# A fused attention and mixture-of-experts kernel: the attention's pieces in another written order

## The chip, the cores and the metric

The kernel runs on one core of a Trainium2 chip. The metric is the device time of one execution in microseconds (us). A core has five engines, each with its own instruction stream that it works through in order: TensorE (PE; its weight loads are shown as PEld), VectorE (DVE), ScalarE (ACT), GpSimd (POOL) and SyncE (SP, which here issues most transfers).

## The reference, cut to what matters

Shapes: q, k and v are 8 batches x 8 heads x 576 tokens x 64. Attention has two parts that are added; the result, as 4608 rows of 512, goes through a mixture of 8 experts, one expert per row.

```python
# part 1: all against all, on means over 4 neighbouring tokens (144 of 576), repeated 4 times
out_d = sm_attn(q_d, k_d, v_d);  out_up = np.repeat(out_d, 4, axis=2)
# part 2: each token against those less than 4 away
scores = np.where(np.abs(pos[:, None] - pos[None, :]) < 4, scale * q @ k.T, -1e9)
out_local = softmax(scores) @ v
x = (out_up + out_local).transpose(0, 2, 1, 3).reshape(4608, 512)
# experts: logits, argmax, gate = softmax weight of the chosen one
e_idx = np.argmax(x @ w_gate + modality_bias[modality_id], axis=1)
out[rows of e] = gate * (np.maximum(x[rows of e] @ w1[e], 0) @ w2[e])
```

## The kernel before, in words

**Attention** (class `Attention`) works in 32 steps n, four per batch: a step is two of the batch's heads, as two halves of the partitions. Its pieces, by their names in the code, are: `tpq` and `tpk` transpose queries and keys on PE, `tpt` does the odd rest of two steps; `qT` and `kT_` copy them out of PSUM on ACT; `kd` sums the keys by fours on DVE, from the same PSUM tile that `kT_` copies; `qe` and `qd` sum the queries by fours on POOL. `mk` and `sc` put the mask and the local scores of half a step into PSUM, `lm` and `le` take the maximum and subtract it on DVE, `exp` is on ACT, `z` and `zr` sum and invert on DVE, `nl` normalises on POOL, `lt` transposes on DVE, the four `Pw_` copies on ACT write the block form, and `avl` multiplies by the values on PE. The coarse part has `scd`, `dm`, `de`, `nd`, `pdt`, `PdT`, `avd` and `Od`; `vp` and `vc` make its values. `X` adds both parts on DVE.

**Routing** (class `Router`) runs per batch, some three steps behind: `lg`, `LT`, `lgt`, `L`, `ch1`, `ex`, `ch2`, `gt`, `pr`, `pl`, the table scatters `st` on POOL's queue, the transposes `R` on DVE and their stores `W` on SP's queue.

**Experts** come last: units of gathered rows, two matrix products each. The first unit begins within the last attention steps.

What sets the order: `build` gives every piece a time, in steps, from the table `PHASE` (n + phase for a piece of step n, 4b + phase for a piece of batch b), sorts all calls by it and records them in that order under a manual schedule. Each engine then holds its instructions in that order, and waits where a tile is not ready. Loads of q, k and v are calls too; their places were worked out from other entries: a query and key load from the latest of the three transposes, a value load from the later `avl`. PSUM tiles stand in four small rings (3 buffers for `tp`, `tpt`, `vp`, `pdt`, `lgt`; 3 for `sc` and `scd`; 2 for `avd`, `avl`, `lg`, `pr`). After attention's last pieces another scheduler orders the expert stage.

Of the kernel before, what the change touches and what calls it, by code (L numbers as in the profile page):

```python
# [20 lines left out]
B, H, S, D = 8, 8, 576, 64  # L21
# [174 lines left out]
class Attention:  # L196
# [114 lines left out]
    def kd(s, n, i):  # L311
# [9 lines left out]
        else:  # L321
            p = s.t.pop(("tp", "k", n)).rearrange("m (t x) -> m t x", x=4)
# [154 lines left out]
class Router:  # L477
# [116 lines left out]
    def R(s, b, t):  # L594

        if t < s.t["G", b]:
            if t % 2 == 0:
# [586 lines left out]
def build(tc, q, k, v, mid, w_gate, bias, w1, w2, out):  # L1184
    nc = tc.nc
    with ExitStack() as ctx:
# [10 lines left out]
        with ExitStack() as actx:  # L1197
# [40 lines left out]
            last = max(P["tpq"], P["tpk"], P["tpt"])  # L1238
            used = max(P["avl0"], P["avl1"])
            batch = ("lg", "LT", "lgt", "L", "ch1", "ch2", "ex", "gt", "pr", "pl", "st", "R", "W")  # L1240
            for b in range(B):
                call(4 * b + min(P[x] for x in P if x[:2] in ("lg", "R0")), lambda b: ro.begin(b, X[b]), b)
            for nm, p in P.items():
                f, i = (nm[:-1], int(nm[-1])) if nm[-1].isdigit() and nm not in ("ch1", "ch2") else (nm, 0)
                if f in batch:
                    for b in range(B - 1):
                        late_ = {2: 0.05, 0: 0.9, 3: 0.14}.get(i, 0) if f == "st" and b == B - 2 else 0
                        call(4 * b + p + late_, getattr(ro, parts.get(f, f)), b, i)
# [339 lines left out]
```

## Time and profile before

| | |
|---|---|
| Median of 3 runs | 667.54 us (667.39 to 668.28) |
| The profiled execution, its own time | 669.48 us |
| Its span, first to last instruction | 667.8 us |
| Mean granted TensorE clock | 0.987 of full |
| Busy: PE, DVE, ACT, POOL | 624.9, 444.2, 387.2, 337.7 us |
| Attention ends (last X) | 256.0 us |

The span has three parts. Up to some 30 us the first loads arrive. The attention steps follow, up to 256 us. From there PE does expert matmuls to the end. A row of the trace gives an engine, a source line, an operation, and out<-in by the names above.

### The profile page before, as it was taken

To read this page: it belongs to the slowest core of one execution; us is meant where nothing else is said; L and a number is where in the kernel's file an instruction comes from. 1 tells how busy PE (TensorE), PEld (TensorE's weight loads), DVE (VectorE), ACT (ScalarE), POOL (GpSimd) and SP (SyncE) were. 2 spreads that over 40 slices of the span, in tenths; PEclk is the share of its full clock that TensorE was granted. 3 is DMA by queue.
4 is the path that set the end of the run, shared out by engine and by line. 5 is a ranking of instruction groups with operands and counts; after the bars stand their busy time and mean duration, and the time that the engine had idled before them with its cause. 6 is when DMAs were issued, how large, how long until landed. Compare 5 with 4: busy or idle time off the path is not lost. (4 is left out here: it accounts for less than half of the span.)

```text
span 667.8 us, 16270 instructions
## 1 busy us (share of the span) xinstructions
PE 624.9 (94%) x5987; PEld 493.9 (74%) x5987; DVE 444.2 (67%) x977; ACT 387.2 (58%) x902; POOL 337.7 (51%) x376
## 2 busy tenths in 40 slices
PE   6798989987998879999999999999999999999996
PEld 4566666765766657888888888888888888889894
DVE  7688898989898985744346673766737967225540
ACT  5698989987898862422354642446324464335540
POOL 7544645627376747343049876498764730113102
PEclk9899999998999997999999999999999999999998
DMA  9999898798899856277002435234341234537801
GB/s 183 164 183 185 162 181 178 153 195 166 171 157 218 165 148 153 87 177 187 16 32 103 107 85 161 53 103 107 90 155 68 79 111 143 173 111 204 242 1 45
DMA packets 178012, 90.21 MB, mean 135 GB/s; under 512 B 144036, under 2 KB 162506, under 8 KB 177930
## 3 DMA queue, kind: packets, MB, share of 16 engines
q1 hardware_dynamic: 169994, 69.96, 48.7%
q0 software_dynamic: 7936, 19.18, 9.3%
q8 instruction: 48, 0.79, 0.6%
q14 instruction: 34, 0.28, 0.2%
HBM read 69.86 MB, written 19.51 MB: 134 GB/s over the span
## 5 line engine op out<-in xcount | busy, mean ns | idle before, releaser
L1045 PE MATMUL l<-V,H 128*128 128x512 f32 x804 | 190.0, 395 | 0.0
L1045 PEld LDWEIGHTS l<-V,H 128*128 128x128 f32 x804 | 150.2, 188 | 34.7
L923 POOL DMA_INDIRECT xg<-xs,m x64 | 74.8, 1169 | 19.2 <-issue 18.6
L405 POOL TENSOR_TENSOR le<-le,zr 128x384 f32<-128x384 f32 x32 | 26.7, 834 | 88.8 <-DVE zr L401 76.8
L1055 POOL DMA_INDIRECT out_dram<-o,tq x24 | 28.7, 1194 | 79.9 <-ACT o L1047 61.9
L992 PE MATMUL l<-X,H 128*128 128x512 f32 (+1 forms) x264 | 58.9, 375 | 0.0
L421 ACT COPY Pw<-lt 32x288 f32<-32x288 f32 x128 | 54.6, 426 | 3.7 <-DVE lt L416 2.1
L1047 ACT ACTIVATE o<-l,tq 128x512 f32<-128x512 f32 x24 | 16.5, 689 | 68.6 <-PE l L1045 43.7
L992 PEld LDWEIGHTS l<-X,H 128*128 128x128 f32 x264 | 45.7, 193 | 9.2 <-issue 1.0
L621 POOL DMA_INDIRECT tab<-ig,si x36 | 38.7, 1075 | 19.0 <-DVE pn L745 12.8
L1148 ACT ACTIVATE H<-o 128x512 fp32r<-128x512 f32 x36 | 22.8, 634 | 39.7 <-DVE o L1170 39.6
L460 PE MATMUL avl<-Pw,vw 128*64 128x96 f32 x768 | 40.2, 254 | 5.7 <-ACT Pw L421 5.6
L460 PEld LDWEIGHTS avl<-Pw,vw 128*64 128x64 f32 x768 | 33.6, 139 | 13.6 <-ACT Pw L421 8.3
L1055 POOL DMA_INDIRECT out_dram<-o,tg x12 | 13.6, 1137 | 55.7 <-ACT o L1047 40.1
L860 DVE TENSOR_TENSOR V<-raw,V 128x1024 fp32r<-128x1024 f32 x23 | 34.4, 1512 | 7.1 <-ACT V L854 7.0
L391 ACT ACTIVATE de<-scd,dm 128x144 f32<-128x144 f32 x96 | 35.4, 377 | 5.4 <-DVE dm L383 3.4
L309 ACT COPY kT<-tp 64x512 f32<-64x512 f32 x64 | 37.0, 579 | 2.4 <-PE tp L277 1.6
L997 ACT ACTIVATE H<-l 128x512 fp32r<-128x512 f32 x24 | 14.4, 598 | 36.5 <-PE l L992 36.0
L998 DVE SCALAR_TENSOR_TENSOR H<-l,H 128x512 fp32r<-128x512 f32 x24 | 16.5, 690 | 28.5 <-ACT H L997 28.4
L351 PE MATMUL sc<-kT,qT 128*24 128x64 f32 x1536 | 34.5, 223 | 1.0 <-ACT kT L309 1.0
L351 PEld LDWEIGHTS sc<-kT,qT 128*24 128x24 f32 x1536 | 24.5, 103 | 11.0 <-issue 4.6
L378 PE MATMUL scd<-kd,qd 64*64 64x144 f32 x384 | 31.1, 295 | 1.4 <-DVE le L364 1.4
(277 smaller groups left out, 1421.2 us busy)
## 6 DMA issues: line engine op xcount, KB each, us to landing
raw<-in_moe_w_dram SPq DMA_DIRECT2D x112, 128.0 KB
raw<-in_moe_w_dram SPq DMA_DIRECT2D x28, 512.0 KB
vw<-in_v_dram SPq DMA_DIRECT2D x60, 180.0 KB
qt<-in_q_dram SPq DMA_DIRECT2D x30, 288.0 KB
kt<-in_k_dram SPq DMA_DIRECT2D x30, 288.0 KB
xs<-R SPq DMA_DIRECT2D x56, 128.0 KB
xs<-G SPq DMA_DIRECT2D x8, 128.0 KB
xg<-xs,m POOLq DMA_INDIRECT x64, 3.0
```

Source lines behind the costliest of these rows:

```text
L309: s.nc.scalar.copy(s.kB[r, g, a, PAD + 64 * g : PAD + 64 * g + 512], p[r])
L351: s.nc.tensor.matmul(p[32 * j : 32 * j + SUB, 2 * i : 2 * i + 2, :], qT[:, q0 : q0 + SUB], kB[:, :, q0 : q0 + WIN], start=False, stop=(i = ...
L378: s.nc.tensor.matmul(p[r, c, :], qd[r, 40 * c : 40 * c + 64], kd[r, :], start=True, stop=True, skip_group_check=True)
L391: s.nc.scalar.activation(x, s.t["scd", n][:, c].rearrange("p (k x) -> p k x", k=NB), AF.Exp, bias=m[:, c : c + 1], accum_out=s.t["z", n][: ...
L421: s.nc.scalar.copy(s.Pw[n % NPW][r, :, j, :SUB], s.t["lt", n][r, :, :SUB])
L460: s.nc.tensor.matmul(p[64 * a : 64 * a + 64, c], vw[:, NB * (4 * (hp // 2) + hp % 2 + 2 * a) + k, :], Pw[:, 2 * k + a], start=True, stop=T ...
L621: i = nc.gpsimd.indirect_dma_start(out=s.tab[:, :], out_offset=bass.IndirectOffsetOnAxis(ap=C.si[:, t : t + 1], axis=0), in_=C.ig[:, t, :] ...
L860: (nc.gpsimd if turn == 4 else nc.vector).tensor_tensor(lo, raw, hi.bitcast(F32), op=ALU.subtract)
L923: s.nc.gpsimd.indirect_dma_start(out=R[l].rearrange("p h (i x) -> p (h i) x", i=4)[:, i, :], out_offset=None, in_=s.xs.rearrange("n (a x) ...
L992: nc.tensor.matmul(p[:, f % n, :], a[:, fs], x[:, k, :N], start=(k == 0 and i == 0), stop=(k == 3 and i == 2))
L1045: nc.tensor.matmul(p, l, x[:, f % 2, :], start=(f == 0 and i == 0), stop=(f == 7 and i == 2))
L1055: nc.gpsimd.indirect_dma_start(out=s.out[:, :], out_offset=bass.IndirectOffsetOnAxis(ap=T[:, h, 0:1], axis=0), in_=o, in_offset=None, boun ...
```

## The change

The table `PHASE` holds new numbers for every piece. Three rules of `build` go with it. The loads have entries `qk` and `v` of their own, with the values that were worked out before (0.4388 and 3.8377). The scatters of the last batch but one are placed by `nd`, `nl` and `pl`. A batch's first use is found over `lg` and all `R`. In `kd` the tile is no longer taken out of the dictionary, so that `kd` may be written before `kT_`; in `R` the tile of two transposes is made by whichever comes first. Both programs hold the same instructions in the same number.

```diff
 PHASE = {
-    "tpq": 0.0000, "tpk": 0.0000, "qT0": 0.0000, "mk0": 0.0000, "tpt": 0.1888, "kT0": 0.2050, "qT1": 0.5097,
...
+    "tpq": 0.0000, "tpk": 0.0054, "tpt": 0.0286, "kd0": 0.0860, "qT0": 0.1020, "kT0": 0.1281, "qT1": 0.3104,
...
 }
...
-            p = s.t.pop(("tp", "k", n)).rearrange("m (t x) -> m t x", x=4)
+            p = s.t["tp", "k", n].rearrange("m (t x) -> m t x", x=4)
...
-            if t % 2 == 0:
+            if ("R", b, t // 2) not in s.t:
...
-            last = max(P["tpq"], P["tpk"], P["tpt"])
...
-                call(4 * b + min(P[x] for x in P if x[:2] in ("lg", "R0")), lambda b: ro.begin(b, X[b]), b)
+                call(4 * b + min(P[x] for x in P if x[:2] == "lg" or x[0] == "R"), lambda b: ro.begin(b, X[b]), b)
...
-                        late_ = {2: 0.05, 0: 0.9, 3: 0.14}.get(i, 0) if f == "st" and b == B - 2 else 0
-                        call(4 * b + p + late_, getattr(ro, parts.get(f, f)), b, i)
+                        at_ = 4 * b + p
+                        if f == "st" and b == B - 2:
+                            at_ = {2: max(N - 2 + P["nd"], 4 * b + P["pl"]) + 0.0001, 0: N - 1 + P["nl"] + 0.0001, 3: N - 0.865 + P["nd"]}.get(i, N + 2.2)
+                        call(at_, getattr(ro, parts.get(f, f)), b, i)
...
-                        call(4 * b - 1 + used + 0.3 + 0.8 * j, at.load_v, b + 1, 4 * j)
+                        call(4 * b - 1 + P["v"] + 0.8 * j, at.load_v, b + 1, 4 * j)
...
-                call(2 * h - 5 + last + 0.25, at.load_qk, h // 2, h % 2)
+                call(2 * h - 5 + P["qk"], at.load_qk, h // 2, h % 2)
```

Line numbers after the table are one higher in the changed kernel. DVE in the step in which the routing of the batch before runs, from the reciprocal of the sums (`zr`) to the first routing piece (`L`), before:

```order
L401 RECIPROCAL zr<-zr 128x15
L606 STREAM_TRANSPOSE R<-X 128x512
L323 TENSOR_REDUCE kd<-tp 128x128
L358 TENSOR_REDUCE lm<-sc 128x6
L364 TENSOR_TENSOR le<-sc,lm 128x192
L526 TENSOR_REDUCE L<-lgt 128x16 x2
```

and in the changed kernel:

```order
L607 STREAM_TRANSPOSE R<-X 128x512
L401 TENSOR_SCALAR zr<-z 128x15
L402 RECIPROCAL zr<-zr 128x15
L365 TENSOR_TENSOR le<-sc,lm 128x192
L324 TENSOR_REDUCE kd<-tp 128x128
L359 TENSOR_REDUCE lm<-sc 128x6
L417 STREAM_TRANSPOSE lt<-le 128x384
L527 TENSOR_REDUCE L<-lgt 128x16 x2
L365 TENSOR_TENSOR le<-sc,lm 128x192
```

Here `R` moved ahead of the sums, the first `le` moved between the reciprocal and `kd`, and `lt` ahead of the second `le`; a maximum and its subtraction no longer stand next to each other.

ACT in the same step, from the queries' copy (`qT`) to the exponentials of the scores (`le<-le`), before:

```order
L297 ACTIVATE qT<-tp 128x512
L514 COPY LT<-lg 128x256
L309 COPY kT<-tp 64x512 x2
L514 COPY LT<-lg 128x256
L421 COPY Pw_166<-lt 32x12x24 x3
L450 ACTIVATE Od<-avd 128x144
L540 ACTIVATE ex<-L 128x32
L369 ACTIVATE le<-le 128x384
```

and in the changed kernel:

```order
L515 COPY LT<-lg 128x256 x2
L422 COPY Pw_166<-lt 32x12x24
L298 ACTIVATE qT<-tp 128x512
L310 COPY kT<-tp 64x512 x2
L422 COPY Pw_166<-lt 32x12x24
L541 ACTIVATE ex<-L 128x32
L451 ACTIVATE Od<-avd 128x144
L422 COPY Pw_167<-lt 32x12x24
L370 ACTIVATE le<-le 128x384
```

Both `LT` copies moved ahead of `qT`, and two of the three `Pw` copies that stood behind `kT` moved ahead of `qT`.

PE in the same step, from the mask (`sc<-mask`) ahead of the router's logits (`lg`) to the local values (`avl`), before:

```order
L343 MATMUL sc<-mask,identb 128x192
L507 MATMUL lg<-X,wg 32x256 x8
L351 MATMUL sc<-kT,qT 24x64 x12
L520 MATMUL lgt<-ident,LT 128x128 x4
L445 MATMUL avd<-PdT,vd 64x144 x4
L378 MATMUL scd<-kd,qd 64x144 x6
```

and in the changed kernel:

```order
L508 MATMUL lg<-X,wg 32x256 x8
L278 MATMUL tp<-ident,qt 128x128 x4
L278 MATMUL tp<-ident,kt 128x128 x4
L344 LDWEIGHTS identb
L344 MATMUL sc<-mask,identb 128x192
L352 MATMUL sc<-kT,qT 24x64 x12
L521 MATMUL lgt<-ident,LT 128x128 x4
L379 MATMUL scd<-kd,qd 64x144 x6
L446 MATMUL avd<-PdT,vd 64x144 x4
```

`lg` moved ahead of the step's transposes, so that these and a mask stand between `lg` and `lgt`, and `scd` moved ahead of `avd`.

## Rows read from the trace of the kernel before

**Rows 1.** The page: busy time by engine; the table scatters (busy, mean ns, idle before)

```profile
PE 624.9 (94%) x5987; PEld 493.9 (74%) x5987; DVE 444.2 (67%) x977; ACT 387.2 (58%) x902; POOL 337.7 (51%) x376
...
L621 POOL DMA_INDIRECT tab<-ig,si x36 | 38.7, 1075 | 19.0 <-DVE pn L745 12.8
```

**Rows 2.** Busy time by stretch; columns: stretch, its length, busy us by engine, clock, DMA

```profile
30.43:60.07 29.64, 26.07 (x511) 19.34 (x512) 24.06 (x75) 26.37 (x85) 11.70 (x18) 1.00 0.99 190
60.07:88.57 28.50, 26.01 (x516) 19.36 (x513) 25.15 (x79) 25.95 (x82) 15.34 (x20) 1.00 0.96 168
88.57:117.11 28.54, 25.69 (x513) 19.26 (x510) 25.63 (x81) 25.73 (x82) 16.52 (x22) 1.00 0.90 180
117.11:145.82 28.71, 26.20 (x516) 19.49 (x513) 25.29 (x79) 25.98 (x82) 15.19 (x20) 1.00 0.85 169
145.82:178.68 32.86, 27.12 (x511) 20.35 (x510) 29.73 (x105) 25.94 (x81) 16.48 (x22) 0.95 0.94 176
178.68:207.16 28.48, 26.07 (x516) 19.33 (x513) 25.30 (x79) 25.89 (x82) 19.41 (x24) 1.00 0.94 181
207.16:227.66 20.50, 18.52 (x374) 14.02 (x371) 19.11 (x57) 18.53 (x59) 15.97 (x18) 1.00 0.94 162
227.66:256.00 28.34, 22.17 (x329) 15.82 (x328) 22.48 (x64) 17.94 (x53) 15.83 (x17) 0.91 0.63 151
256.00:668.00 412.00, 405.22 (x1901) 332.58 (x1899) 225.93 (x312) 177.37 (x251) 190.83 (x165) 0.99 0.39 112
```

**Rows 3.** Busy time by step of one cycle; order of engines: PE, PEld, DVE, ACT, POOL

```profile
178.68:185.16 6.48, 6.42 (x132) 4.89 (x129) 6.24 (x23) 5.77 (x20) 3.40 (x4) 1.00 0.81 172
185.16:191.30 6.14, 5.50 (x116) 4.22 (x115) 5.90 (x17) 5.92 (x18) 4.93 (x7) 1.00 1.03 161
191.30:197.78 6.48, 6.48 (x129) 4.80 (x129) 5.64 (x15) 6.32 (x22) 4.44 (x7) 1.00 0.66 119
197.78:207.16 9.38, 7.66 (x143) 5.42 (x144) 7.52 (x27) 7.88 (x26) 6.63 (x8) 1.00 1.15 243
```

**Rows 4.** Waits from 178.68 to 207.16: us in total, times, longest

```profile
DVE kd L323 <- ACT kT L309: 2.0, 2, 1.4
...
ACT LT L514 <- PE lg L507: 0.8, 1, 0.8
ACT qT L297 <- PE tp L277: 0.6, 1, 0.6
...
PE lgt L520 <- ACT LT L514: 0.9, 1, 0.9
PE pr L572 <- DVE late L471: 0.7, 1, 0.7
```

**Rows 5.** DVE in order of time, behind the routing step's kd: start, us, line, operation

```profile
202.23 0.35 DVE L358 TENSOR_REDUCE lm<-sc 128x6 f32<-128x192 f32 x1
...
207.13 0.70 DVE L606 STREAM_TRANSPOSE R<-X 128x512 f32<-128x512 f32 x1
...
209.22 0.19 DVE L584 TENSOR_TENSOR sl<-pr,ecap 128x40 f32<-128x40 f32 x1
...
210.35 0.65 DVE L606 STREAM_TRANSPOSE R<-X 128x512 f32<-128x512 f32 x1
210.92 0.65 DVE L323 TENSOR_REDUCE kd<-tp 128x128 f32<-128x512 f32 x1
```

**Rows 6.** Busy time from one kT to the next, and ACT's second LT in it

```profile
200.41:208.34 7.93, 6.40 (x131) 5.04 (x123) 6.38 (x23) 6.50 (x20) 4.34 (x6) 1.00 1.18 251
...
201.61 0.43 ACT L514 COPY LT<-lg 128x320 f32<-128x320 f32 x1
```

**Rows 7.** Busy time in the stretch at half clock

```profile
251.20:258.00 6.80, 6.49 (x33) 4.83 (x34) 3.19 (x7) 1.04 (x3) 6.55 (x5) 0.50 0.46 92
```

**Rows 8.** SP's issue of a pair's query load, and PE's first use of it

```profile
148.88 1.20 SPq L233 DMA_DIRECT2D qt<-in_q_dram  x2
...
178.68 0.60 PE L277 MATMUL tp<-ident,qt 128*128 128x128 f32 x4
```

More of the change, by code (lines that the diff above doesn't have):

```diff
@@ L1241, in build @@
             for b in range(B):
-                call(4 * b + min(P[x] for x in P if x[:2] in ("lg", "R0")), lambda b: ro.begin(b, X[b]), b)
+                call(4 * b + min(P[x] for x in P if x[:2] == "lg" or x[0] == "R"), lambda b: ro.begin(b, X[b]), b)
             for nm, p in P.items():
+                if nm in ("qk", "v"):
+                    continue
                 f, i = (nm[:-1], int(nm[-1])) if nm[-1].isdigit() and nm not in ("ch1", "ch2") else (nm, 0)
```

19 rows, old and new, of the table PHASE are left out of this document.

## The prediction

> **What bounds the kernel now.** I read the page's busy shares first, then busy time by stretch, then one cycle of the attention stage step by step, then the waits of that cycle. The page gives PE 94% of the span [rows 1], which looks like a bound engine. The stretches say where that holds: from 256 us on the routed-expert stage keeps PE busy nearly throughout, and the table that changes holds no piece of it. Before that lie the 32 attention steps, and in them three engines stand close together: over the four steps from 178.68 to 207.16 DVE is busy 25.30, ACT 25.89 and PE 26.07 of 28.48 us [rows 2]. No engine is full; each loses 2.4 to 3.2 us per four steps to waits for the other two. So the order of work, and not an amount of work, sets the length of this stage, and what the stage gives back goes straight to the end, because PE works without a break behind it.
>
> The four steps are not alike [rows 3]. The first three take 6.48, 6.14 and 6.48 us with at most 0.84 us of idle DVE or 0.71 of idle ACT. The fourth, in which the routing of an earlier batch runs, takes 9.38 us with DVE busy 7.52 and ACT 7.88: there the time is lost.
>
> How much can go? If in each step the busier of DVE and ACT had no wait, the cycle would be 6.24 + 5.92 + 6.32 + 7.88 = 26.36 us, so its room is 28.48 - 26.36 = 2.12 us [rows 3]. I leave PE out of that sum. In the third step its busy time is the whole step, 6.48 of 6.48, while its weight loads take 4.80 [rows 3]; its matmuls are pipelined and their ends are modelled. Counting PE too, the sum is 6.42 + 5.92 + 6.48 + 7.88 = 26.70 and the room 1.78. The Trainium skill, "Perfetto Trace Analysis", section "Identifying the Most-Contended Engine", says that matmul busy time is a bad measure of how near TensorE is to its limit and that weight-load busy time is a better one; by that rule 2.12 is the room; with PE counted it is 1.78, and the forecast below would be 2.3 us higher. The trace agrees with the rule as far as 4.80 of 6.48 goes.
>
> For all seven stretches from 30.43 to 227.66 the time that the busiest of DVE and ACT stands idle is 3.27, 2.55, 2.81, 2.73, 3.13, 2.59 and 1.39, together 18.5 us [rows 2]. Scaled as in the cycle above (2.12 of 2.59) this is **15.1 us** of room.
>
> **The change, part by part.** No instruction is added or removed; both programs hold the same ones, so busy time stays, and only waits can come and go.
>
> *kd ahead of kT.* Both read the transposed keys of one PSUM tile, and the second reader waits for the first. Before, DVE's kd stood behind ACT's two kT copies and waited 2.0 us per cycle, 1.4 of it in the routing step [rows 4]. Now kd stands before kT, and DVE's wait goes. The price is that kT waits for kd. In the three plain steps I cost this at nothing: ACT has qT ahead of kT, and now two Pw copies ahead of qT, while DVE is the less busy of the two in two of them (5.90 against 5.92, 5.64 against 6.32) [rows 3]. If this cover is gone, each kT waits for at most one whole kd, 0.65 us [rows 5].
>
> *The routing step on DVE.* From the end of one kd to the end of the next DVE works without a wait from 202.23 to 210.92 + 0.65 = 211.57, that is 9.34 us [rows 5]. The change takes out of this interval the two R transposes (0.70 and 0.65) and the four sl and si pieces (4 x 0.19 = 0.76), which now stand behind the next kd or before this one: 7.23 us are left. ACT's work from kT to kT is 6.50 us, less one LT copy of 0.43 that now stands before qT: 6.07 [rows 6]. So ACT will wait some 7.23 - 6.07 = **1.16 us** for kd once per cycle. This is the new wait.
>
> *LT together.* Before, ACT wrote one LT, then the two kT copies, then the other LT, and PE's second pair of lgt transposes waited 0.9 us with avd, scd and avl queued behind it [rows 4]. Now the LT copies follow each other and PE has both tp groups, a mask and a score group between lg and lgt. The lgt wait goes. ACT's 0.8 for lg may stay; it lies in the step where DVE is last, so I take the larger of this and the 1.16, not both.
>
> *pr later.* Before, PE's pr stood ahead of the next step's transposes and waited 0.7 us for DVE, and ACT's qT waited 0.6 behind it [rows 4]. Now pr stands behind tp, mk and tpt, a quarter of a step later. Both waits go; what is late next is DVE itself, which is the 1.16 again.
>
> *POOL.* The score normalisation nl and nd now come some 0.4 of a step earlier against pdt, and the table scatters have moved to either side of them. POOL is busy 19.41 of 28.48 us even in the cycle that also holds gathers [rows 2], so I cost the scatters at nothing. If one met an nl that was due, DVE's lt would wait up to its 1.08 us [rows 1], once a cycle.
>
> *Loads and stores on SP.* The two load offsets now have entries of their own, with the sums that were computed before (0.1888 + 0.25 and 3.5377 + 0.3), so the loads keep their place in the step. A pair's query load is issued at 148.88 and used at 178.68 [rows 8]: 30 us of cover, of which the forecast uses less than a microsecond per cycle. Two of the R transposes are written 0.2 of a step later and three earlier; the last store of a batch comes one and a half steps earlier, right behind its transposes. SP will wait there for DVE, with the next loads queued behind it under the same cover, so I cost this at nothing.
>
> *Ends.* The first 30 us wait for the first loads; I take no gain. The last stretch, 227.66 to 256, has 22.48 us of DVE work in 28.34 and mixes the last steps with the first expert matmuls; the pieces there move too, in no clear direction: 0, with 2 us to either side.
>
> **The sum.** Per cycle: room 2.12 less the new wait 1.16 is 0.96 us. Seven stretches, the last three quarters of a cycle long, are 6.75 cycles: 6.75 x 0.96 = 6.5 us. The profiled execution took 669.48 us by its own time, so 663.0 on its scale; it lies 1.94 above the median of the runs shown, 667.54, and on the median's scale the forecast is **661.0 us**. The bounds: all the room goes and the 1.16 hides under DVE, 667.54 - 15.1 = 652.4; or as many waits come as go, 667.5.
>
> **The rivals.**
>
> *All the room goes*, 652.4 us. For it: in the routing step DVE is last, and a wait of ACT there costs nothing if the buffers let ACT catch up in the next three steps. Against: in the third step ACT has 0.16 us of idle time [rows 3], so nothing can be caught up there.
>
> *The waits only change places*, 667.5 us. For it: kd behind kT becomes kT behind kd, and three engines at 90% leave little slack. Against: four different waits of the routing step [rows 4] are taken up at once, and only one new one is seen.
>
> *kT behind kd makes ACT the ring's slowest link*, slower than before. The place is ACT's first kT copy; behind it are Pw and so avl, and the scores of the step. If DVE reaches kd late in the plain steps too, each costs up to 0.65, so a cycle pays 3 x 0.65 + 1.16 = 3.11 against the 2.0 of kd's wait that is gone: +1.11 by 6.75 cycles is +7.5, or 675.0 us. It decides from the point at which DVE, behind z, lm, zr, the reciprocal and le, ends kd later than ACT ends qT. Against: DVE's busy time is below ACT's in the second and third step. For: by 0.02 us in the second, and in the first it is above it, 6.24 against 5.77 [rows 3].
>
> *The clock.* At 251.2 to 258 the granted clock is 0.50, the 1.2 GHz level, with PE busy 6.49 of 6.80 us on the first expert matmuls [rows 7]; ahead of it, in the last attention steps, PE was busy 22.17 of 28.34 [rows 2]. If a fuller end of the attention kept the 2.4 GHz level, this PE work would take half its time: another -3.2 us, 657.8 us. The Trainium skill, "TensorE: Matmul & The Clock Gate", section on the HAM clock gate, calls the slow level the default that activity releases, which is this mechanism; the trace has the slow level behind 6.17 us of idle PE time in one stretch, and agrees. Against: the last steps depend on each other as before, and little of the change lies there; and a new gap elsewhere would cost as much.
>
> **How the numbers follow.** Chances: the forecast 0.52, all the room 0.12, the clock on top 0.09, waits that change places 0.13, slower 0.14. A measurement of this kernel tells about 0.2% (1.3 us) from no change. Faster is the first three, 0.73; same 0.13; slower 0.14. The range reaches from 652.4 to 668.9, the upper edge of no change; it leaves out the slower case.
>
> **What would show it.** Right: DVE's wait of kd for kT gone from the list of waits, lgt for LT and pr for DVE gone or below 0.3 us; a new wait of ACT's kT for kd, near 1 us and once per four steps; four ordinary steps in about 27.5 us instead of 28.5; PE's stretch without idle time starting some 6 us earlier, and the same length of time behind it. Wrong: kT waiting for kd in most steps; DVE busy under 88% of four steps; or a gain of the attention stage that a longer stretch at 0.50 clock, or a wait of the first expert unit for its weights, takes back.

## The result, and the profile after

The changed kernel is slower by half a per cent: 672.0 us (median of 18 runs, 668.3 to 677.53) against 668.38 for the kernel before in the same comparison (18 runs, 666.28 to 676.95); the ratio is 1.0054 with an interval of 1.0028 to 1.0081. The forecast was 661.0 us, and its range ended at 668.9. Run again beside the experiments, the change took 670.76 us, ratio 1.0045 (1.0022 to 1.0068). Ratios leave out runs in a slower state, over 1.5% above the fastest run of the same kernel, so a ratio can differ from the quotient of two medians.

The page of the changed kernel, the line that answers to [rows 1]:

```profile
PE 633.5 (95%) x5987; PEld 498.0 (75%) x5987; DVE 450.2 (67%) x977; ACT 385.5 (58%) x902; POOL 336.9 (50%) x376
```

The shares are the same within a point. But DVE is busy 6.0 us longer with the same 977 instructions; where that comes from is shown below. The profiled execution took 669.40 us with a span of 667.7, against 669.48 and 667.8 before. Busy time by stretch, cut at the starts of steps 4, 8, 12, 16, 20, 24, 28 and 31, answers to [rows 2] (the columns are those of rows 2):

```profile
31.59:63.46 31.87, 28.48 (x512) 21.45 (x506) 24.46 (x77) 25.64 (x84) 13.44 (x18) 0.89 1.11 188
63.46:90.86 27.40, 26.48 (x517) 19.56 (x511) 25.57 (x78) 25.47 (x82) 15.30 (x20) 1.00 0.92 168
90.86:118.39 27.53, 26.23 (x516) 19.46 (x510) 25.36 (x82) 25.53 (x84) 16.45 (x22) 1.00 0.92 164
118.39:147.35 28.96, 26.87 (x518) 19.68 (x512) 26.72 (x82) 25.84 (x84) 15.12 (x20) 1.00 0.91 180
147.35:175.52 28.17, 26.33 (x518) 19.75 (x511) 27.27 (x102) 25.30 (x81) 16.41 (x22) 1.00 0.94 164
175.52:203.59 28.07, 26.75 (x517) 19.58 (x511) 26.29 (x75) 25.53 (x83) 18.65 (x23) 1.00 0.88 183
203.59:226.77 23.18, 20.89 (x399) 15.12 (x393) 22.05 (x63) 20.56 (x67) 17.14 (x21) 1.00 0.98 188
```

The five whole cycles in the middle are where the prediction looked, and there the change gains: 28.50, 28.54, 28.71, 32.86 and 28.48 us [rows 2] became 27.40, 27.53, 28.96, 28.17 and 28.07, together 6.96 us less. Of this 4.69 us come from the fourth cycle alone, for which nothing special was forecast: before, it holds a stretch at the lower clock, 0.50 of full (0.95 over the cycle; 1.00 after), and 2.5 us more DVE work than after. The gain is lost outside: before step 4 1.16 us (31.59 against 30.43), in steps 4 to 7 2.23 (31.87 against 29.64), in steps 28 to 30 2.68 (23.18 against 20.50), from step 31 to the last X 2.58 (30.91 against 28.33); behind the last X the span is 1.80 us shorter. All together the span is 0.11 us shorter in these two executions. The four steps of the cycle of [rows 3] now read:

```profile
175.52:182.67 7.15, 6.97 (x139) 5.17 (x134) 7.01 (x22) 6.47 (x23) 4.23 (x5) 1.00 0.95 213
182.67:189.08 6.41, 5.64 (x121) 4.28 (x114) 6.38 (x17) 6.00 (x19) 4.30 (x7) 1.00 0.74 140
189.08:196.76 7.68, 7.68 (x151) 5.29 (x145) 6.35 (x19) 7.45 (x27) 4.92 (x6) 1.00 0.82 124
196.76:203.59 6.83, 6.47 (x124) 4.84 (x120) 6.55 (x21) 5.60 (x18) 5.20 (x6) 1.00 1.02 258
```

The routing step's 9.38 us are spread over its neighbours, which are up to 1.2 us longer than before. The waits of this cycle answer to [rows 4]:

```profile
ACT ex L541 <- DVE L L537: 1.1, 1, 1.1
DVE kd L320 <- ACT kT L308: 1.1, 1, 1.1
...
PE avl L461 <- ACT Pw L422: 0.8, 1, 0.8
...
ACT kT L310 <- DVE sl L585: 0.5, 1, 0.5
...
ACT kT L310 <- DVE kd L324: 0.2, 1, 0.2
```

The waits of lgt for LT, of pr for DVE, of LT and of qT that rows 4 show are gone; kT's waits behind DVE sum to 0.7 here. The kd that waits is now the smaller one of the pair (L320), which does not wait in rows 4.

Where the first loss lies, DVE shows in step 5, from 38.19 to 49.02 us. The routing bias is not in the table: it is written at 5.05 by the program itself, behind the sums and ahead of kd, as before; but kT of step 5 stood ahead of kd then and now stands behind it. DVE of the changed kernel in order of time:

```profile
40.16 1.04 DVE L192 TENSOR_TENSOR tb<-m,bb 128x288 f32<-128x288 f32 x1
41.13 0.92 DVE L192 TENSOR_TENSOR R<-m,bb 128x288 f32<-128x288 f32 x1
42.08 0.57 DVE L194 TENSOR_TENSOR tb<-tb,R 128x288 f32<-128x288 f32 x1
42.57 0.35 DVE L365 TENSOR_TENSOR le<-sc,lm 128x192 f32<-128x192 f32 x1
42.84 0.67 DVE L324 TENSOR_REDUCE kd<-tp 128x128 f32<-128x512 f32 x1
```

and ACT beside it:

```profile
39.92 0.60 ACT L298 ACTIVATE qT<-tp 128x512 f32<-128x512 f32 x1
43.62 1.19 ACT L310 COPY kT<-tp 64x512 f32<-64x512 f32 x2 [3.11 <-DVE kd L324]
```

Three bias pieces, 2.5 us together, stand ahead of kd, and ACT's kT, which before needed nothing of DVE, waits 3.11 us. The same three pieces took 0.46, 0.45 and 0.46 us before. There they stood ahead of zr, and POOL, which needs zr for its le, was idle beside them; now zr stands ahead of them and POOL works while they run. The first piece before, and POOL after:

```profile
39.91 0.46 DVE L191 TENSOR_TENSOR tb<-m,bb 128x288 f32<-128x288 f32 x1
```

```profile
39.97 0.92 POOL L410 TENSOR_TENSOR de<-de,zr 128x432 f32<-128x432 f32 x1
```

So some 1.2 us of the 3.11 come from the pieces being longer. The routing's small multiply `sl` shows the same. Before, it took 0.19 or 0.20 us in all eight batches, with POOL idle; in the changed kernel it takes 0.68 to 0.95 us in the seven batches within the attention, each time with POOL's le or de beside it. The second batch, before and after:

```profile
90.85 0.20 DVE L585 TENSOR_TENSOR sl<-sl,oh 128x40 f32<-128x40 f32 x1
```

```profile
93.69 0.91 POOL L410 TENSOR_TENSOR de<-de,zr 128x432 f32<-128x432 f32 x1
...
93.71 0.95 DVE L586 TENSOR_TENSOR sl<-sl,oh 128x40 f32<-128x40 f32 x1
```

Behind step 5's wait follows a stretch at the lower clock, which the kernel before does not have here:

```profile
43.90:50.70 6.80, 5.39 (x68) 4.84 (x69) 3.45 (x11) 5.54 (x17) 0.69 (x1) 0.50 1.02 187
```

Step 5 takes 10.83 us instead of 6.44.

### The profile page after: what moved, and what is told of

It is laid out like the page before. It is cut to its first block, busy times and chain, and to the rows that moved or that the text cites. A ratio compares the mean times of both kernels' runs of the same rounds, so it can differ in the third digit from the quotient of the medians.

```text
span 667.7 us, 16230 instructions
## 1 busy us (share of the span) xinstructions
PE 633.5 (95%) x5987; PEld 498.0 (75%) x5987; DVE 450.2 (67%) x977; ACT 385.5 (58%) x902; POOL 336.9 (50%) x376
## 5 line engine op out<-in xcount | busy, mean ns | idle before, releaser
L461 PE MATMUL avl<-Pw,vw 128*64 128x96 f32 x768 | 42.9, 258 | 11.1 <-ACT Pw L422 8.9
L861 DVE TENSOR_TENSOR V<-raw,V 128x1024 fp32r<-128x1024 f32 x23 | 36.5, 1606 | 7.3 <-ACT V L855 7.3
L861 DVE TENSOR_TENSOR H<-raw,H 128x1024 fp32r<-128x1024 f32 x12 | 15.3, 1283 | 27.0 <-ACT H L855 23.9
L1110 DVE TENSOR_TENSOR G<-X,G 128x1024 fp32r<-128x1024 f32 x15 | 23.2, 1555 | 12.8 <-ACT G L1109 12.8
```

The lines of the kernel that those rows point to most:

```text
L461: s.nc.tensor.matmul(p[64 * a : 64 * a + 64, c], vw[:, NB * (4 * (hp // 2) + hp % 2 + 2 * a) + k, :], Pw[:, 2 * k + a], start=True, stop=T ...
L861: (nc.gpsimd if turn == 4 else nc.vector).tensor_tensor(lo, raw, hi.bitcast(F32), op=ALU.subtract)
```

## The experiments

The runs were taken in sets, and each set has its own runs of the kernel before, against which its ratios stand. The table gives the lead over the kernel before, in us, at the start of steps 8, 20, 28 and 31, at the end of the last X and at the end of the span, from the profiled execution of each kernel (minus: behind), and the ratio of the timed runs. The kernel before stands at 60.07, 145.82, 207.16, 227.66, 255.99 and 667.78. A row of leads is one execution, which can lie apart from the median of its kernel: that of e2 is the slowest of its 12 (674.14 us, median 669.75), that of f2 the fastest of its 6 (674.15, median 680.06); the others lie within 3.3 us of their medians.

| kernel | 8 | 20 | 28 | 31 | last X | end | ratio (interval) |
|---|---|---|---|---|---|---|---|
| change | -3.4 | -1.5 | 3.6 | 0.9 | -1.7 | 0.1 | 1.0054 (1.0028 to 1.0081) |
| e1 | 1.9 | 3.9 | 3.9 | -0.8 | -2.3 | -0.4 | 1.0025 (0.9998 to 1.0052) |
| e2 | -2.7 | -1.6 | 1.4 | -6.4 | -5.0 | -4.6 | 1.0029 (1.0010 to 1.0049) |
| e3 | 1.9 | 3.5 | 7.9 | 0.7 | -2.8 | 0.6 | 1.0000 (0.9971 to 1.0029) |
| f1 | 0.6 | 2.6 | 7.4 | 6.1 | -2.4 | 1.6 | 1.0005 (0.9985 to 1.0024) |
| f2 | 1.6 | 3.6 | 8.7 | -6.2 | -8.7 | -4.7 | 1.0176 (1.0138 to 1.0215) |
| c1 | -0.7 | -0.4 | 0.1 | -6.0 | -6.2 | -4.8 | 1.0035 (1.0006 to 1.0063) |
| k1 again | 1.4 | 3.0 | 8.5 | 4.8 | 1.5 | 0.7 | 0.9986 (0.9967 to 1.0005) |

**The fixed pieces.** The change unedited, and three runs on it:

> The changed kernel once more, to see what differs between executions. If its time against the kernel before comes from fixed places, the same waits as in the first profile return: ACT's kT waits some 3 us for kd at step 5 (near 40 us), a half-clock stretch follows near 44 us, DVE waits some 2.5 us for POOL's H near 244 us, and the time is 3 to 4 us above the kernel before. If the order as such makes the time uncertain (rival: clock alone), the half-clock stretches lie elsewhere and these waits differ by over 1 us.

In e0 step 5 is as in the first profile: its bias pieces take 1.05, 0.92 and 0.56 us, and the step 10.25.

```diff
-            call(5.05, C.biases, tc, cp, work, at.wk, ps)
+            bias = C.biases(tc, cp, work, at.wk, ps)
+            for x in (4.40, 5.40, 6.40):
+                call(x, next, bias, None)
```

> The router's bias table (3 us of DVE work, written at a fixed 5.05, now between a step's maximum and kd) is cut into three parts, each behind a step's dm. Theory A (fixed pieces written ahead of kd hold ACT's kT): the 3.1 us wait of kT for kd in step 5 falls below 1 us, the half-clock stretch at 44 us goes, step 8 starts at 59 to 61 us instead of 63.5, and the time falls by 3 to 5 us against the changed kernel. Rival B (the tail alone makes it slower): step 8 may start earlier, the time stays within 1 us of the changed kernel.

The second places the last weight splits where they stood before; `nd` has fallen from 2.5956 to 2.1531 and had drawn them with it:

```diff
-            end = N - 1 + P["nd"] + 0.12
+            end = N - 1 + 2.5956 + 0.12
```

> The last four weight pieces keep their place of before (31 + 2.5956 + 0.12) instead of following nd to 33.27. Theory B: DVE's 2.5 us wait for POOL's H at 244 us and PE's 2.6 us wait of pdt behind it go, the last X ends 1.5 to 2.5 us earlier against the start of step 31, and the time falls by 1.5 to 2.5 us. Theory A alone: no more than 0.5 us. Rival (the pieces are needed there by the first expert unit): PE waits for H or V between 256 and 265 us and nothing is won.

> Both edits. If both places cost what they seem to, the sum: 5 to 7 us below the changed kernel, so 2 to 4 us below the kernel before (about 664 us). If the order as such is slower (rival), no better than the kernel before.

With the biases cut, kT of step 5 follows qT at once:

```profile
39.98 0.60 ACT L301 ACTIVATE qT<-tp 128x512 f32<-128x512 f32 x1
40.59 1.18 ACT L313 COPY kT<-tp 64x512 f32<-64x512 f32 x2
```

Step 5 is 5.67 us, the stretch at the lower clock is gone, and e1 is 5.3 us ahead of the change at step 8 and 5.5 at step 20. The time is 670.03 against 670.76 for the change in the same set: of 5 us in the stage hardly one arrives, which is what the rival said, and the two are not told apart. In the execution of e1, POOL waits 6.5 us in step 27 for the early unit's first gather, and the lead falls from 8.6 us at step 24 to 3.9 at step 28. e2 shortens the stretch from step 31 to the last X from 29.90 us (e0) to 26.86, but half of that is lost behind the last X, and its time, 669.75, is not told from the change either. On top of e1 the same edit does not shorten this stretch: 29.89 us in e1, 31.78 in e3. Both edits together give 668.65 us, 2.1 under the change beside it and not told from the kernel before (ratio 1.0000). So together they make up for the loss, as far as such intervals tell, with e1's edit seen in the steps and e2's not shown by itself; the 664 us that were expected did not come. And e3 is 7.9 us ahead at step 28, and of this nothing is left at step 31.

**The raw weights.** In these four runs step 30 takes 12 to 14 us. In the first profile of the change it took 8.82, the raws were issued at 210.4 us instead of 216.9 in e0, and POOL did not wait for them; so this wait differs from execution to execution. POOL of e0, in order of time:

```profile
220.16 1.01 POOL L622 DMA_INDIRECT tab<-ig,si  x1 [0.15 <-issue]
224.98 1.03 POOL L855 CAST H<-raw 128x1024 fp32r<-128x1024 f32 x1 [3.81 <-DMA vw<-in_v_dram]
225.99 0.90 POOL L410 TENSOR_TENSOR de<-de,zr 128x432 f32<-128x432 f32 x1
```

and the waits from 218 to 234 us:

```profile
DVE H L861 <- POOL H L855: 4.3, 1, 4.3
ACT PdT L439 <- PE pdt L431: 4.2, 1, 4.2
...
PE pdt L431 <- POOL de L410: 2.1, 1, 2.1
```

POOL reaches the cut of the early expert's first raw weights 3.8 us before they are there (this row names the values' transfer, the same row in e3 the raws'); DVE's other half of the cut, POOL's de, PE's pdt and ACT's PdT stand behind it. f1 is e3 with these cuts written later, f2 is e3 with the loads written earlier, and c1 is the control: the kernel before with the loads written later.

```diff
 f1
-                    call(w + 1.5 + 0.6 * c + 0.25 * j, wsplit, c)
+                    call(w + 2.5 + 0.3 * c + 0.15 * j, wsplit, c)
 f2
-                call(w - 1.5 + 0.5 * c, wload, c)
+                call(w - 3.4 + 0.5 * c, wload, c)
 c1 (in the kernel before)
-                call(w - 1.5 + 0.5 * c, wload, c)
+                call(w - 0.5 + 0.5 * c, wload, c)
```

> This is e3_both (biases cut, the last two pieces of the weight split kept at their old place) with the first two weight splits (POOL's CAST H<-raw and DVE's H<-raw,H) written 0.4 to 1.0 step later, so that POOL has two more de, one qe, one qd and one le ahead of the first cast. Theory 1, the raw weights arrive too late for the place at which they are cut, and POOL and DVE stand behind them: step 30, 13.4 us in e3_both, comes down to 8 to 9, and the time falls by 3 to 5 us against e3_both's 668.65, to 663.5 to 665.5. Rival, the transfers themselves bound the attention (DMA share 0.9 to 1.1 over 140 to 230 us in the kernel before too): the wait moves on to the next thing that is loaded and step 30 plus step 31 together shrink by under 1.5 us; time 667 to 669.

> This is e3_both with the four raw weight loads written 1.9 steps earlier, ahead of the last values' loads and of the stores of batch 4; the cuts stay. Theory 1 (only the raws are late): the raws land some 10 us earlier (SP issues them before 203 us instead of 212 to 218), POOL's cast in step 30 waits for nothing, step 30 is 7 to 9 us and the time 663 to 665.5. Rival (transfers bound the attention): what stood ahead of the raws, the last values or the stores, comes as much later; vp or the gathers then wait and steps 28 to 31 together shrink by under 1.5 us; time 667 to 669.

> This is the kernel before with nothing changed but that the four raw weight loads are written one step later, behind the last values' loads; SP then issues them some 10 us later, as the change lets them come in its own time scale. If the raws' lateness against the cuts is what costs step 30 its 6 us, it shows here without any other part of the change: POOL's first cast waits 3 to 6 us, DVE's subtraction behind it, step 30 grows from 7.0 to 10 to 13 us, and the time rises by 2 to 5 us, to 670.5 to 673. If the lateness is harmless by itself, step 30 stays at 7 to 8 us and the time within 1 us of before.

c1 shows the wait in a kernel that has no other part of the change (waits from 218 to 234 us):

```profile
POOL H L854 <- DMA raw<-in_moe_w_dram: 5.7, 1, 5.7
...
PE pdt L430 <- POOL de L409: 5.2, 2, 4.9
```

Its step 30 takes 13.14 us instead of 7.04 and its time is 671.07 against 668.49. So late raws alone are enough to make step 30 as long as it is in e0. In f1 the wait is gone and step 30 is 7.47 us, as expected; the time, 668.16, is what the rival said: step 31 to the last X takes 36.81 us there instead of 31.78 in e3. f2 took 680.06 us, far above both expectations. SP's issues there, in its fastest execution:

```profile
196.21 1.88 SPq L834 DMA_DIRECT2D raw<-in_moe_w_dram  x4
...
208.19 8.93 SPq L834 DMA_DIRECT2D raw<-in_moe_w_dram  x12
217.17 6.40 SPq L257 DMA_DIRECT2D vw<-in_v_dram  x5
```

and the wait on PE that follows, between 20 and 256 us:

```profile
PE vp L269 <- DMA vw<-in_v_dram: 11.1, 1, 11.1
```

What was put ahead pushed the last values back, and vp waited 11.1 us for them: the rival's mechanism, at a price that it did not have. Compare SP in the kernel before:

```profile
208.09 3.21 SPq L830 DMA_DIRECT2D raw<-in_moe_w_dram  x4
211.40 3.22 SPq L615 DMA_DIRECT2D xs<-R  x4
214.81 2.69 SPq L830 DMA_DIRECT2D raw<-in_moe_w_dram  x4
...
223.80 0.34 SPq L253 DMA_DIRECT2D vw<-in_v_dram  x1
```

and in f1:

```profile
211.44 4.44 SPq L834 DMA_DIRECT2D raw<-in_moe_w_dram  x8
...
221.54 0.34 SPq L257 DMA_DIRECT2D vw<-in_v_dram  x1
```

The attention of f1 is 7.4 us ahead at step 28, the last values are issued 2.3 us earlier, and the first raws 3.3 us later. SP issues with gaps of at most 0.2 us from 208.09 to 217.50 us in the kernel before. These rows fit a reading in which the stage's loads come at their own pace and a faster attention meets them earlier; the next runs test parts of it. The Trainium skill, "Perfetto Trace Analysis", section "What 'DMA-bound' means", names an issuing engine whose track is solid with transfers as one of the forms of being bound by them; the rows of SP agree with it for this stretch.

**What makes the raws late.** n3 is e3 with three of the four raw blocks not loaded, n2 the same in the kernel before; h1 puts the stores that the change moved ahead of the values back, on e3, and h2 on f1.

```diff
 n3, n2
-                raw.append(moe.wload(E[0][0], c))
+                raw.append(raw[0] if 0 < c < 4 else moe.wload(E[0][0], c))
 h1, h2
-    "R2": 9.5091, "R3": 9.5731, "W1": 9.5838, "st1": 10.0627,
+    "R2": 9.5091, "R3": 9.5731, "W1": 11.1000, "st1": 10.0627,
...
-            w = max(t + 5, 4 * (B - 2) - 1 + used + 1.1 + 0.8)
+            w = 28.4377
```

> This is e3_both with only the first of the early expert's four raw weight blocks loaded; the three others are cut out of that first block, so three quarters of these weights are not the expert's own and 1.5 MB fewer are moved (at some 180 GB/s that is 8 us of transfers, an estimate from the stretch 140 to 180 us). Everything else, the cuts' places and all work of the engines, is as in e3_both. Theory, the transfers hold the end of the attention once it runs ahead: POOL's wait for the raws goes, step 30 falls from 13.4 to 7 to 8 us, the 8 us of lead at step 28 last to the end, and the time is 660 to 664. Rival, the end is held by the engines' own work and the clock: step 30 gets shorter, what is gained is lost behind it as in f1_casts_later, and the time is 666 to 669.

> This is the kernel before with the same three raw blocks not loaded and cut out of the first. It is the control: if in the kernel before the engines, not the transfers, set the pace of the attention, the 1.5 MB are worth nothing there, the steps stay within 1 us each of what they are and the time is 666.5 to 669. If the transfers hold the kernel before as well, it falls by 3 to 8 us, to 660 to 665, and the difference between the two kernels is not due to them.

> This is e3_both with the stores W1 back at 11.1000 (the change has 9.5838) and the raws' loads and cuts at the kernel before's time (28.4377 for w instead of 28.6335). On SP the values' loads and the raws then stand ahead of four stores again. Theory, SP's order makes the raws late: SP issues them by 207 us instead of 212, POOL's first cast waits under 1 us instead of 3.8, step 30 is 7 to 9 us instead of 13.4, and the time 663.5 to 666.5 against 668.65. Rival, the raws come as late because all transfers ahead of them are late: they are issued at 210 us or later, step 30 stays over 11 us, time 667.5 to 669.5.

> This is f1_casts_later with the same stores and raws put back. f1 has no wait for raws, so if SP's order matters only through the raws, this is worth nothing: 667 to 669. If it also brings the gathers and the last values earlier, and these hold the end, the time falls to 664 to 666.5. A gain in h1 and none here would say that raws were all of it.

n2 and n3 leave three quarters of these weights out and serve for their times alone. n3 took 672.59 us (ratio 1.0028, 0.9998 to 1.0057), above both expectations and not told from the kernel before. Its one raw block was still issued at 212.5 us (212.2 in e3) and POOL still waited 4.6 us: what delays the first block is what stands ahead of it, not the bytes of the others. n2 took 665.97 (0.9976, 0.9953 to 0.9999). Its steps start within 0.7 us of those of the kernel before up to step 31; the gain comes at the end, where the clock stays up ([rows 7] has 0.50 in the same stretch):

```profile
251.20:258.00 6.80, 6.80 (x48) 4.99 (x47) 2.34 (x5) 0.37 (x2) 6.29 (x5) 1.00 0.58 117
```

h1 took 672.13 (1.0068, 1.0043 to 1.0093). The raws were issued from 210.2 us on, POOL waited 3.6 us, step 30 took 13.31: the rival's signs, in a time that is worse than either said. h2 took 668.33 (1.0010, 0.9986 to 1.0034), no better than f1. So putting this part of SP's order back does not take the wait away. That the order costs nothing is not shown: in n3, h1 and h2 POOL also waits 5 to 6 us in step 27 for the early unit's first gather, as in e1, and not in e3 and f1, from which they start. One thing is clear of noise: h2 and h1 differ only in the place of the cuts, were run in one set, and h2 is 3.8 us faster. There the wait for the raws does cost time to the end.

**The end of the attention.** In f1, DVE's subtractions stand ahead of the routing chain of step 31; ACT waits 2.5 us for that chain, PE 1.74 for ACT's Od, and a stretch at the lower clock begins at 231.3 us. g1 puts the cuts behind the chain; h3 repeats the mask matmul of step 31 so that PE has something to do ahead of those waits (the numbers written are the same).

```diff
 g1
-                    call(w + 2.5 + 0.3 * c + 0.15 * j, wsplit, c)
+                    call(w + 3.1 + 0.3 * c + 0.15 * j, wsplit, c)
 h3
-        s.nc.tensor.matmul(p, s.C.identb, s.mask if x else s.C.mask, start=True, stop=False, skip_group_check=True)
+        for r in range(16 if n == 31 else 1):
+            s.nc.tensor.matmul(p, s.C.identb, s.mask if x else s.C.mask, start=True, stop=False, skip_group_check=True)
```

> This is f1_casts_later with the first two weight splits written another 0.6 step later, so that DVE's two subtractions (1.92 and 1.23 us in f1_casts_later) come behind the routing chain of step 31 (L, mx, ex, oh) and no longer ahead of it. In f1_casts_later ACT waits 2.5 us for that chain (ex<-L) and so PE 1.74 us for Od, and the half clock of 231.3 to 238.1 us follows. Theory, what is lost at the end of the attention is DVE's and POOL's queue there, and the clock that falls behind its waits: the waits go, at most one half-clock stretch is left between 220 and 260 us, and the time is 664.5 to 667. Rival, the end of the attention is held by something else (the transfers, or the early unit's own work): the waits move to the later cuts and the time is 667 to 669.

> This is f1_casts_later with the mask matmul of step 31 (128x192, bf16, 0.08 us each when it runs in a row) issued 16 times instead of once at its two places, ahead of the two waits of 1.74 and 1.55 us behind which the half clock of 231.3 to 238.1 us begins; it writes the same numbers each time. If the clock takes the lead away, that stretch goes, PE's work from 231 to 240 us takes 3 us less, and the time is 664.5 to 666.5 against 668.16. If not, the 2 us of extra matmuls fill waits and cost nothing or up to 1 us, and the time is 667.5 to 669.5.

g1 took 671.06 us (1.0040, 1.0016 to 1.0063), above what either said; its profiled execution, 667.15, is the fastest of its nine and does not show why. In h3 the clock did as was meant. First f1, then h3, the same stretch:

```profile
231.30:240.00 8.70, 8.35 (x101) 5.59 (x100) 6.73 (x19) 3.40 (x12) 2.73 (x3) 0.61 0.91 224
```

```profile
231.30:240.00 8.70, 8.02 (x150) 5.92 (x146) 7.53 (x25) 5.17 (x19) 2.73 (x3) 1.00 0.86 237
```

and the time was 667.62 (1.0012, 0.9984 to 1.0040), the time for the case that the clock does not matter, and not told apart from f1's 668.16. But in the profiled execution of h3 POOL waits 5.4 us in step 27 for the early unit's first gather, whose small table stands on SP behind values; f1's waits 0.5. A stretch of 3.4 us at the lower clock, which f1 does not have, follows at 202.6, and the lead at step 28 is 4.8 instead of 7.4, so the two are not a clean pair and the price of the clock stays open. k1 (on f1) and k2 (on h3) write these gathers one step later:

```diff
-                call(t + 4.75 + 0.3 * i, rows, 0, i)
+                call(t + 5.75 + 0.3 * i, rows, 0, i)
```

> This is f1_casts_later with the early unit's four gathers (POOL's xg<-xs,tg) written one step later, so that they no longer stand ahead of qd of step 27 when their table has not landed. Theory, every transfer behind which POOL stands takes lead away: POOL's wait of up to 6 us and step 27's 8 to 10 us go (step 27 at 6.8 to 7), the lead at step 28 is 8 us in every execution, the time 664.5 to 666.5 and the spread smaller. Rival, the end of the attention takes the lead whatever it is: the time is 667 to 669.5.

> This is h3_clock_held (the mask matmul of step 31 repeated, f1's cuts) with the same four gathers one step later. If waits for transfers and the clock behind them are together what takes the lead, this is the fastest of all: 663.5 to 666. If k1 alone falls and this is no better than k1, the clock is worth nothing here; if neither falls, the end of the attention is bound by the engines' own work and the change can't be turned into a gain in this way.

> k1_gathers_later once more, without a change. If the kernel before is at its usual 668 us: theory, POOL's wait for the gather's table is gone, step 27 is 6.8 to 7 us, the lead at step 28 is 8 us and the time is 664.5 to 666.5; rival, the end of the attention takes the lead whatever it is, and the time is 667 to 669.5. If the kernel before is again near 678, transfers are slow there and nothing is told apart.

In the set of k1 and k2 the kernel before itself took 677.85 us (668.69 to 681.49); k1 took 679.09 (1.0062, 1.0019 to 1.0104) and k2 678.05 (1.0057, 1.0016 to 1.0099). SP issued k1's last values at 235.06 us instead of f1's 221.54:

```profile
235.06 0.34 SPq L257 DMA_DIRECT2D vw<-in_v_dram  x1
```

and vp waited 4.7 us for values. The kernel before and k1 are some 10 us slower there than in the other sets, so that set tells nothing of the gather. In another set, k1 again took 667.64 (0.9986, 0.9967 to 1.0005): step 27 is down to 6.17, the lead at step 28 is 8.5, and the time is again that of the kernel before, as the rival said.

**kd's place.** e4 is the change with `kd0` back behind kT at 0.3000, e5 the kernel before with `kd0` at 0.1900, ahead of kT.

```diff
 e4
-    "tpq": 0.0000, "tpk": 0.0054, "tpt": 0.0286, "kd0": 0.0860, "qT0": 0.1020, "kT0": 0.1281, "qT1": 0.3104,
+    "tpq": 0.0000, "tpk": 0.0054, "tpt": 0.0286, "kd0": 0.3000, "qT0": 0.1020, "kT0": 0.1281, "qT1": 0.3104,
 e5 (in the kernel before)
...
-    "kT1": 0.5356, "sc0": 0.5591, "qe": 0.6232, "qd": 0.6242, "lm0": 0.7343, "le0": 0.8414, "kd0": 0.3000, "kd1": 0.5400,
+    "kT1": 0.5356, "sc0": 0.5591, "qe": 0.6232, "qd": 0.6242, "lm0": 0.7343, "le0": 0.8414, "kd0": 0.1900, "kd1": 0.5400,
...
-            p = s.t.pop(("tp", "k", n)).rearrange("m (t x) -> m t x", x=4)
+            p = s.t["tp", "k", n].rearrange("m (t x) -> m t x", x=4)
```

> This is the change with kd0 alone put back behind kT (0.3000 instead of 0.0860). If kd ahead of kT is what gives the cycle its 1 us, the steady cycles from step 8 to step 28 lengthen from 28.0 to some 28.5 each, DVE waits for kT at kd again (14 us in the kernel before over the attention, 6 in the change), ACT waits for kd nowhere, and step 5 falls from 10.8 to 8 us or less, since ACT no longer stands behind the biases: time 669 to 672. If kd's place is worth nothing by itself, the cycles stay at 28.0 and only step 5 gets shorter: time 667 to 669.5.

> This is the kernel before with kd0 alone written ahead of kT (0.1900). If that order is the whole of the gain in the cycles, the cycles of 28.5 us become 27.5 to 28, and since step 5 gets the wait of ACT behind the biases only if they stand ahead of kd (they are written at 5.05, kd of step 5 now at 5.19), step 5 grows by 1 to 4 us: time 664 to 668. If the cycle's gain needs the other moves of the table, the cycles stay at 28.5 and ACT's wait for kd replaces DVE's wait for kT: time 667 to 671.

e4 took 674.19 (1.0092, 1.0067 to 1.0118), above what was expected: its first two cycles from step 8 take 28.02 us each, against 27.40 and 27.53, and step 5 falls to 7.04, behind a step 4 of 11.89, in which PE waits 2.4 us for a key load. So kd ahead of kT is worth 0.5 to 0.6 us in each of these two cycles of the new table. In the old one it is a loss: e5 took 687.49 (1.0288, 1.0262 to 1.0314), far outside both expectations. Its waits from 64.7 to 193.5 us:

```profile
PE avl L460 <- ACT Pw L421: 13.9, 12, 2.2
ACT kT L309 <- DVE zr L400: 9.8, 9, 2.3
```

There DVE reaches kd behind X, lm, le and z of the steps before (kd is written ahead of zr, with which the row names the end of the wait), kT waits, Pw stands behind kT and PE's avl behind Pw. This is the mechanism of the prediction's slower rival, at a higher price; the rest of the table is what makes kd's place pay.

## Why the prediction was wrong

*The cycle.* Right in kind, smaller in size. Room less one new wait gave 0.96 us per cycle; measured were 1.10, 1.01, -0.25, 4.69 and 0.41. The average of 1.39 is luck: without the fourth cycle, in which the search for the early unit runs on DVE, it is 0.57. The four waits of rows 4 that were to go went (the small kd waits instead, up to 1.1 us a time), and kT's waits behind DVE (kd and sl) sum to 4.4 us from 60 to 200 us, some 0.9 per cycle where 1.16 was forecast.

*"Both programs hold the same ones, so busy time stays."* It did not. To the last X, DVE's 666 instructions take 222.5 us of busy time where they took 218.2 before, and the bias pieces and `sl`, which now run beside POOL, are among those that grew. `sl`, which the sum moved out of the routing step at its old 0.19 us, takes some 0.75 us more where it stands now.

*The sum over 6.75 cycles.* This is the first step that failed. A cycle from the middle was taken for all seven stretches, the first and the last with it. The first holds the biases, written at a fixed 5.05 ahead of kd, which cost nothing as long as kT needed no kd; it lost 2.23 us, and with the biases cut (e1) this stretch is 3.1 us shorter than before the change (26.57 against 29.64). The rule "kT waits nothing in the plain steps" holds where DVE has nothing but the table's pieces ahead of kd.

*"Ends: 0, with 2 us to either side."* The last stretch lost 2.58 us, but the expert stage behind it gave 1.80 back, so 0.8 are left, within what was allowed. Of the pieces placed by `nd`, e2 showed 3.0 us in that stretch and e3 none. Before step 4 another 1.16 us went, beside a stretch at the lower clock that is twice as long (6.8 us instead of 3.4); that was not tried by itself.

*"30 us of cover, so I cost this at nothing."* True of the queries that were looked at, and read as if it held for all loads. The raw weights and the gather's table are loaded with a few microseconds to spare: c1 shows that raws issued 9.4 us later cost step 30 6.1 us. An attention that is 7 us ahead uses such cover up. The DMA column of [rows 2], 0.85 to 0.99 in the seven stretches to 227.66, could have been read as a warning; n3, with 1.5 MB fewer to move and no gain, does not show that it was one. The move of the stores on SP was costed at nothing: h1 and h2 gain nothing by putting it back.

*"What the stage gives back goes straight to the end."* This is the step that failed last, and it holds the whole forecast. f1 and k1 again are 7.4 and 8.5 us ahead at step 28 and 6.1 and 4.8 at step 31, where 6.5 were forecast; 1.6 and 0.7 are left at the end, and their times are not told from the kernel before. PE's work behind the attention has no break, but the attention's last steps already hold the early expert's weights, gathers and first products, and there the lead is used up.

*The rivals.* The slower case had its mechanism at ACT's first kT copy, and it is that place where step 5 stalls, but behind a piece that the rival did not name; over the cycles it does not occur. The clock came in with the other sign at step 5. The prediction's own list of what would prove it wrong had the early expert's wait for its weights, without a price.

*What stays open* is why the lead does not reach the end. With the biases cut, the last splits kept, the first splits and the gathers moved (k1 again), the time is at best 0.1% under the kernel before. Part of it is seen: in e3, f1, g1, h1, h2, h3 and k1 again the stretch from step 31 to the last X takes between 31 and 37 us instead of 28.3, with more of the early expert's first product done inside (17 records of it in h3 against 4 before), and in f1 and k1 again with some 13.6 us at the lower clock against 6.8 before. The profiled execution of the kernel before also lies 1.1 us above its median in the comparison, so that its leads are overstated by as much. Which of these takes the rest was not settled, and no version that does all of the work beats the kernel before by more than its interval.

## What to carry to other kernels

A gain per cycle holds only where the cycle repeats. List what is placed by a fixed number or by a derived one (here the biases and the last splits), and look at it with the new order around it. Then follow the lead to the first thing that comes at its own pace: for every load, not one, take the time from landing to use, and where it is smaller than the gain, move the use or expect the wait. Moving a piece also changes what runs beside it: a duration read from the old order is not safe in the new one (`sl`: 0.20 us with POOL idle, 0.95 beside its de). An order that pays in one table can cost several per cent in another (kd: 0.5 us in a cycle gained here, 2.9% lost there).

## What the runs showed of the hardware

A POOL cast and a DVE subtraction of the same size lengthen each other when they overlap. POOL of f1, two casts of 128x1024:

```profile
223.08 1.04 POOL L858 CAST H<-raw 128x1024 fp32r<-128x1024 f32 x1
...
224.93 2.03 POOL L858 CAST H<-raw 128x1024 fp32r<-128x1024 f32 x1
```

The second runs beside DVE's subtraction, which starts at 224.15 and takes 1.92 us where others take 1.23. The Trainium skill, "SBUF — State Buffer", section "Who interferes with whom", says that a DVE instruction with two SBUF inputs contends with a GpSimd instruction that reads SBUF; the rows agree, and the price here is about 1 us for the cast and 0.7 for the subtraction. The rows of `sl` and of the bias above agree as well: `sl` starts 0.02 us behind POOL's de and ends 0.06 behind it, 0.95 us for a piece that takes 0.20 with POOL idle. No run takes POOL's work away with all else kept, so this rests on the times alone.

The time of the same kernel differed by 9.4 us between two sets (kernel before, 668.41 and 677.85), and by at most 1 us between all the others (667.85 to 668.82). k1 lost 11.5 us along with it, and SP issued its last values at 235.06 us there and at 226.38 in k1 again. The sets ran on different chips, and within the set of 677.85 single runs of the kernel before took 668.69 to 681.49; what makes the difference is not shown.
